# The products of the experts' second matrices as two 64-row tiles of TensorE

## The chip, the cores and the metric

The kernel runs on one core of one Trainium2 chip. Its time is the device time of one execution in microseconds (us); less is better. A core has five engines with instruction queues of their own: TensorE (PE in the profile, with its weight loads listed apart as PEld), VectorE (DVE), ScalarE (ACT), GpSimd (POOL) and SyncE (SP). TensorE multiplies a stationary matrix (the weights, loaded ahead of each product) with a moving one and adds the products up in PSUM, a small memory of eight banks of 128 x 512 floats. Only VectorE and ScalarE read PSUM.

## What is computed

The reference is a sparse attention whose output goes through a mixture of experts with fixed capacity. Cut to what matters:

```python
# attention: q, k, v are (8, 8, 576, 64)
scores = scale * q @ k.T
scores = where(scores >= max(scores) - tau, scores, -1e9)
x = softmax(scores) @ v               # laid out as 4608 tokens x 512
# routing: the best (token, expert) pairs first, 576 tokens for each of 8 experts
logits = x @ w_gate
for idx in argsort(-logits.flatten()):
    tok, e = idx // 8, idx % 8
    if assigned[tok] < 0 and counts[e] < 576: assigned[tok] = e; counts[e] += 1
# experts
for e in range(8):
    h = maximum(x[assigned == e] @ w1[e], 0)      # 576x512 @ 512x1024
    out[assigned == e] = h @ w2[e]                # 576x1024 @ 1024x512
```

## The kernel before

**Two phases.** Until about 480 us attention runs; then come eight rounds, one expert each. A round finds its expert's 576 tokens by a search over thresholds (class `Router`, lines 503 to 547: comparisons on VectorE, counts by small matmuls), gathers their rows (line 780), scales and transposes them (line 806) and runs the two matrices of the expert, `ffn`. Search, gather and transposes of later rounds run while `ffn` of an earlier round keeps TensorE busy, and their small matmuls stand between its products.

**Number format.** Both matrices work on float32 split into a high and a low part (`w1h`, `w1l`, `w2h`, `w2l`, and in `H` the same for the hidden values), each in the reduced format F32R, which TensorE takes in one pass. A product needs three matmuls: high by high, high by low and low by high. Attention works on full float32, which TensorE takes in two passes, each with a record of its own in the trace.

**First matrix.** Line 865: for each of eight blocks of 128 hidden rows, 24 matmuls of mostly 288 columns, into a PSUM tile `pf` of two banks. ScalarE takes the rectified values out (line 877) and rounds them to the high part, VectorE subtracts to get the low part (all VectorE work of this phase has line 426, a helper that also keeps the planner's clock).

**Second matrix.** Line 897: for each of five blocks of 128 tokens, in the order 0, 4, 1, 2, 3 (`L2O`), eight hidden blocks f times three matmuls with all 128 rows and 512 columns, 24 in all, added up in the first bank of a `pf` tile. The other bank lies idle. Block 4 holds the high and the low part of the last 64 tokens side by side and needs 16 matmuls; its halves are added later with the help of a DMA (`y5`, `z5`). Line 900: ScalarE copies the bank to `y`. Line 905: GpSimd issues an indirect DMA that scatters the rows to the output. Eight rounds have 8 x (4 x 24 + 16) = 896 of these matmuls.

**Order of the work.** The program's order on every engine is written out by a planner in the kernel itself: generators yield estimated times, `ffn` is the one that paces the plan, and `jobs` are the others. Small VectorE jobs are put into a list `fills` by `later(key, work)`. A function `flush` takes them out once they are 7 us old or VectorE is free, the search takes one at each of its gaps, and `want(key)` takes one out on the spot when the work that follows needs it. PSUM holds two `pf` tiles (two banks each), two tiles for transposes and two for the search and the packing.

The attention's scores (line 69) already go in two tiles of 64 rows: each of the two matmuls of a head takes 64 of the 128 partitions and a bank of its own.

Of the kernel before, what the change touches and what calls it, by code (L numbers as in the profile page):

```python
# [9 lines left out]
F32 = mybir.dt.float32  # L10
# [4 lines left out]
ALU = mybir.AluOpType  # L15
# [686 lines left out]
def moe(ctx,tc,R,start,xrows,w1,w2,out,ident):  # L702
    nc=tc.nc
    V=R.V; A=nc.scalar; G=nc.gpsimd; T=nc.tensor
    E,D,F=w1.shape
    w1p=ctx.enter_context(tc.tile_pool(name="mw1",bufs=1))
    wk=ctx.enter_context(tc.tile_pool(name="mwk",bufs=1))
# [2 lines left out]
    st={}  # L710
    done=set()

    fills=[]
    def later(k,g): fills.append((clk[0],k,g))
    def pull(k=None):
        if fills:
            i=next((i for i,x in enumerate(fills) if x[1]==k),None)
            if i is None: i=next((i for i,x in enumerate(fills) if x[1][0] in ("hl","w2l","w2")),0)
            _,k,g=fills.pop(i); g(); done.add(k)
# [119 lines left out]
    def ffn(r,s):  # L839
        H=wk.tile([128,8,2*CAP],F32R,name="H")  # L840
        def want(*k):
            while k not in done:
                if any(x[1]==k for x in fills): pull(k)
                else: yield k


        blocks=[(f,(0,1)) for f in range(8)]
        if r==0: blocks[:2]=[(0,(0,)),(1,(0,)),(0,(1,)),(1,(1,))]
        elif r<=HALF: blocks[:1]=[(0,(0,)),(0,(1,))]
        cols=(slice(0,256),slice(256,576)) if r==0 else (slice(0,HS),slice(HS,2*HS))  # L850
        pss={}
        for f,hs in blocks:
            if 0 in hs:
                if r>0 and f==4: yield from want("w1a",r)
                if f>=HFB: yield from want("hl",r,f-HFB)
                pss[f]=pf.tile([128,2,512],F32,name="pf")
            ps=pss[f]
            if hs==(1,): yield ("x",r)
            ops=[(k,j) for j in range(3) for k in range(4)] if r==0 else [(k,j) for k in range(4) for j in range(3)]
            for i,(k,j) in enumerate(ops):  # L860
                w,x=(("w1h","xh"),("w1h","xl"),("w1l","xh"))[j]
                if r==0 and (k,j)==(0,2): yield ("w1l",f)
                for h in hs:
                    n=cols[h].stop-cols[h].start
                    T.matmul(ps[:,h,:n],s[w][:,k,f*128:(f+1)*128],s[x][:,k,cols[h]],start=(i==0),stop=(i==11))  # L865
                if i<11: yield (0.25 if r==0 and hs==(0,) else 0.132)*len(hs)
            if 1 not in hs: yield 0.132; continue
            two=lambda a: a.rearrange("p (a b) -> p a b",a=2)
            hT=two(H[:,f,0:512]); hL=two(H[:,f,512:576]); lL=two(H[:,f,576:640]); lT=two(H[:,f,640:1152])
            hf=wk.tile([128,2,HS],F32,name="hf",bufs=HFB)  # L870
            if r==0:
                hv=hf.rearrange("p a b -> p (a b)")
                hT,hL,lL,lT=H[:,f,0:512],H[:,f,512:576],H[:,f,576:640],H[:,f,640:1152]; v0,v1=hv[:,0:512],hv[:,512:576]
                for h in range(2): A.activation(hv[:,cols[h]],ps[:,h,:cols[h].stop-cols[h].start],AF.Relu)
            else:
                v0,v1=hf[:,:,0:256],hf[:,:,256:288]
                A.activation(hf,ps[:,:,:HS],AF.Relu)  # L877
            A.activation(hT,v0,AF.Copy); A.activation(hL,v1,AF.Copy)
            def low(f=f,a=((lT,hT,v0),(lL,hL,v1))):
                yield LOWT  # L880
                gp=r in LOWP and f<LPF
                def work():
                    for l,h,v in a: (G if gp else V).tensor_tensor(l,v,h.bitcast(F32),op=ALU.subtract)
                if gp: work(); done.add(("hl",r,f))
                else: later(("hl",r,f),work)
            jobs.append([clk[0],low()])
            yield 0.25
        done.add(("l1",r))
        for t in L2O:
            ps=pf.tile([128,2,512],F32,name="pf")  # L890
            ops=(((576-64,"w2h"),(576-64,"w2l")) if t==4 else ((t*128,"w2h"),(t*128,"w2l"),(640+t*128,"w2h")))
            for f in range(8):
                yield from want("hl",r,f)
                yield from want(*(("w2l",r,f) if f<7 else ("w2",r)))
                for j,(c,w) in enumerate(ops):
                    e=(f==7 and j==len(ops)-1)
                    T.matmul(ps[:,0,:],H[:,f,c:c+128],s[w][:,f],start=(f==0 and j==0),stop=e)  # L897
                    if not e: yield 0.227
            y=wk.tile([128,D],F32,name="y5",bufs=1) if t==4 else wk.tile([128,D],F32,name="y",bufs=2)
            A.activation(y,ps[:,0,:],AF.Copy)  # L900
            if t==4:
                if r>0: yield from want("y5",r-1)
                y5=y; z=wk.tile([64,D],F32,name="z5",bufs=1); nc.scalar.dma_start(z,y[64:128])
            def store(t,y,n):
                G.indirect_dma_start(out=out,out_offset=IOA(ap=s["idx"][:n,t:t+1],axis=0),in_=y[:n],in_offset=None)  # L905
            if t<4: store(t,y,128)
            if t==(L2Z if r==7 else 2):
                def last(y5=y5,z=z,store=store):
                    V.tensor_tensor(y5[0:64],y5[0:64],z,op=ALU.add); store(4,y5,64)
                if r==7: last()  # L910
                else: later(("y5",r),last)
            yield 0.227
        done.add(("l2",r))
# [44 lines left out]
    for r in range(8):  # L958
        while not all((n,r) in done for n in ("w1","half" if r<=HALF else "x")):
            now+=0.25; run(now)  # L960
        for d in ffn(r,st[r]):
            if type(d) is tuple:
                while d not in done:
                    now+=0.25; run(now)
                    if d not in done and any(x[1]==d for x in fills): pull(d)
                continue
            held[0]=0.0; now+=d; run(now); now+=held[0]; clk[0]=now
# [35 lines left out]
def build(tc, qk, vl, tau, wgd, cst_d, w1, w2, out, off, nb=8):  # L1003
    nc=tc.nc
    with ExitStack() as ctx:
        ctx.enter_context(tc.manual_schedule())
        cp=ctx.enter_context(tc.tile_pool(name="cst",bufs=1))
        dr=ctx.enter_context(tc.tile_pool(name="dr",bufs=1,space=bass.MemoryType.DRAM))
        xrows=dr.tile([8*S,XW],F32,name="xrows")
        xts=dr.tile([8,128,4,S],F32,name="xts")  # L1010
        ident=cp.tile([128,128],F32,name="ident"); make_identity(nc,ident)
        dup=cp.tile([128,128],F32,name="dup")
        for a in range(2): nc.vector.tensor_tensor(dup[:,64*a:64*a+64],ident[:,0:64],ident[:,64:128],op=ALU.add)
        Lg=cp.tile([128,NC_,8],F32,name="Lg")
        cst=cp.tile(list(cst_d.shape),F32,name="cst")
        R=Router(ctx,tc,cst,off,Lg)
        def load_cst(): nc.sync.dma_start(cst,cst_d)
        with ExitStack() as actx:
            start=attention(actx,tc,qk,vl,tau,wgd,xrows,xts,Lg,nb,ident,dup,R,load_cst)
        pp=ctx.enter_context(tc.tile_pool(name="rp",bufs=1,space=PSUM))  # L1020
        R.ps=lambda t=pp.tile([128,512],F32,name="rps"): t
        R.cp=lambda t=pp.tile([128,512],F32,name="cps"): t
        moe(ctx,tc,R,start,xrows,w1,w2,out,ident)
# [15 lines left out]
```

## Time and profile before

| | |
|---|---|
| time, median of 3 runs | 968.95 us (968.77 to 970.25) |
| the profiled execution | 967.75 us, span 966.0 us |
| mean granted TensorE clock | 0.989 |
| VectorE, ScalarE, GpSimd busy | 80%, 66%, 28% of the span |
| line 900, ScalarE, y from pf | 40 times, 598 ns |
| line 905, output stores on GpSimd | 40 times |
| a round of the experts, rounds 1 to 3 | about 60 us |
| the last round's second matrix | 931 to 956.6 us |

A line of the profile names the source line, the engine, the operation, output and inputs with their shapes, the count, the busy time in us and the mean duration in ns. For TensorE the shape in front, 128\*128 or 64\*128, is the rows and columns of the array that the instruction uses: 64\*128 is a tile of half height. Matmuls overlap in TensorE's pipeline, so a duration is longer than the distance from one start to the next.

### The profile page before, as it was taken

What the parts mean: (1) busy time and instruction counts of PE and PEld (TensorE: products, weight loads), DVE (VectorE), ACT (ScalarE), POOL (GpSimd) and SP (SyncE); (2) the same over time, 40 slices, a digit from 0 to 9 for tenths busy, and PEclk for the clock granted to TensorE, in tenths of its full rate; (3) what the DMA queues carried; (4) which work ended last, traced back from release to release, by engine and by line L of the source; (5) the groups of instructions that cost most, each with busy time, mean ns of one, the idle gap of its engine ahead of it and who ended that gap; (6) DMA issues with size and microseconds to landing.
All of it is one profiled execution on the core that took longest, in us unless ns stands there. A gap on an engine that the chain in (4) does not pass through costs nothing.

```text
span 966.0 us, 24118 instructions
## 1 busy us (share of the span) xinstructions
PE 938.5 (97%) x9130; PEld 700.3 (72%) x9130; DVE 769.8 (80%) x2134; ACT 638.6 (66%) x1297; POOL 269.0 (28%) x485
## 2 busy tenths in 40 slices
PE   7999999999999999999789999999999999999996
PEld 4556656565566656565688798897988979898994
DVE  8999999999999999996678878687887877536220
ACT  6999999999999999996554354342543525455330
POOL 2435344353434343340020412121111212210101
PEclk9999999999999999999889999999999999999998
DMA  6332253532533323205751516143343425431101
GB/s 259 108 115 88 86 184 103 197 134 100 179 101 111 125 100 125 88 2 204 251 169 65 198 59 187 52 138 126 109 149 127 137 95 186 163 98 34 40 12 43
DMA packets 35861, 117.00 MB, mean 121 GB/s; under 512 B 4385, under 2 KB 5025, under 8 KB 35233
## 3 DMA queue, kind: packets, MB, share of 16 engines
q1 hardware_dynamic: 28352, 92.85, 27.6%
q0 software_dynamic: 5888, 19.03, 6.2%
q10 hardware_dynamic: 1504, 3.59, 1.2%
q8 instruction: 72, 1.18, 0.5%
q14 instruction: 45, 0.36, 0.1%
HBM read 93.01 MB, written 21.38 MB: 118 GB/s over the span
## 4 chain that ended last, share of the span: by engine, by line
PE 90%; DVE 5%; DMA 2%; issue 2%; ACT 0%; POOL 0%; POOLq 0%; SPq 0%; DVEq 0%
PE pf L865 22%; PE pf L897 20%; PE sc L69 15%; PE xo L155 14%; PE tb L98 8%; PE sc L98 2%; PE xo L165 2%; PE pt L806 2%; DVE pp L90 1%; PE rps L503 1%; DVE z L74 1%; PE xo L177 1%; PE xo L246 1%; DMA out_dram<-y,idx 1%; DVE cmp L426 1%
## 5 line engine op out<-in xcount | busy, mean ns | idle before, releaser
L74 DVE TENSOR_SCALAR_CACHE_REDUCE z<-sc 128x576 f32<-128x576 f32 x288 | 205.9, 751 | 15.4 <-PE sc L69 13.5
L75 POOL TENSOR_SCALAR nb<-nb,taub 128x1 f32<-128x1 f32 x288 | 145.4, 506 | 248.6 <-DVE z L74 185.5
L86 ACT ACTIVATE pp<-z,nb 128x576 f32<-128x576 f32 x256 | 193.1, 773 | 25.2 <-DVE z L74 22.0
L90 DVE SCALAR_TENSOR_TENSOR pp<-z,nb,pp 128x576 f32<-128x576 f32 x256 | 199.9, 813 | 0.0
L897 PE MATMUL pf<-w2h,H 128*128 128x512 f32 x576 | 193.7, 400 | 0.4 <-DVE H L426 0.4
L69 PE MATMUL sc<-qk 64*128 64x288 f32 (+1 forms) x1280 | 178.6, 423 | 1.5 <-DMA qk<-qk_dram 0.7
L155 PE MATMUL xo<-pt,vt 128*64 128x320 f32 (+1 forms) x1024 | 155.9, 420 | 0.0
L116 ACT ACTIVATE pt<-tb 128x512 f32<-128x512 f32 x253 | 137.6, 591 | 1.9 <-PE tb L98 1.4
L897 PE MATMUL pf<-w2l,H 128*128 128x512 f32 x320 | 128.0, 400 | 0.0
L905 POOL DMA_INDIRECT out_dram<-y,idx x40 | 44.8, 1120 | 295.5 <-ACT y L900 251.1
L897 PEld LDWEIGHTS pf<-w2h,H 128*128 128x128 f32 x576 | 106.7, 188 | 22.1 <-DVE H L426 0.8
L69 PEld LDWEIGHTS sc<-qk 64*128 64x128 f32 (+1 forms) x1280 | 93.7, 178 | 28.8 <-DVE z L74 4.3
L865 PE MATMUL pf<-xl,w1h 128*128 128x288 f32 (+2 forms) x512 | 110.4, 301 | 0.0
L865 PE MATMUL pf<-xh,w1h 128*128 128x288 f32 (+2 forms) x512 | 109.7, 300 | 0.7 <-ACT xh L807 0.7
L865 PE MATMUL pf<-xh,w1l 128*128 128x288 f32 (+2 forms) x512 | 109.7, 300 | 0.0
L98 PEld LDWEIGHTS tb<-ident,pp 64*128 64x128 f32 x2032 | 75.0, 139 | 44.9 <-issue 18.9
L900 ACT ACTIVATE y<-pf 128x512 f32<-128x512 f32 x40 | 23.9, 598 | 124.9 <-PE pf L897 117.0
L155 PEld LDWEIGHTS xo<-pt,vt 128*64 128x64 f32 x1024 | 60.6, 136 | 58.5 <-issue 32.4
L877 ACT ACTIVATE hf<-pf 128x576 f32<-128x576 f32 x56 | 36.5, 652 | 89.1 <-PE pf L865 80.8
L98 PE MATMUL tb<-ident,pp 64*128 64x64 f32 x2032 | 91.7, 227 | 3.3 <-ACT pt L116 3.0
L865 PEld LDWEIGHTS pf<-xh,w1h 128*128 128x128 f32 x512 | 82.1, 189 | 1.8 <-ACT xh L807 1.1
L865 PEld LDWEIGHTS pf<-xl,w1h 128*128 128x128 f32 x512 | 81.9, 190 | 0.2
(201 smaller groups left out, 1316.1 us busy)
## 6 DMA issues: line engine op xcount, KB each, us to landing
qk<-qk_dram SPq DMA_DIRECT2D x31, 864.0 KB, 4.6
vt<-vl_dram SPq DMA_DIRECT2D x32, 576.0 KB, 3.8
w2s<-w_dram SPq DMA_DIRECT2D x32, 512.0 KB, 5.5
w1s<-w_dram SPq DMA_DIRECT2D x28, 512.0 KB, 5.8
xrows<-pp SPq DMA_DIRECT2D x24, 260.0 KB, 2.4
xts<-xt SPq DMA_DIRECT2D x2, 1152.0 KB, 5.4
pt<-xts SPq DMA_DIRECT2D x2, 1152.0 KB, 6.2
xrows<-xr SPq DMA_DIRECT2D x8, 260.0 KB, 2.2
```

Source lines behind the costliest of these rows:

```text
L69: T.matmul(sc[o,f,:HS], kd["q",h][r,c], kd["k",h][r,:],start=True,stop=True)
L74: V.tensor_scalar(z,SC.pop(t)[:,:,:HS],-0.125,None,op0=ALU.mult,op1=ALU.min,accum_out=nb[:,0:1])
L75: G.tensor_scalar(nb[:,1:2],nb[:,0:1],taub[:,0:1],None,op0=ALU.add)
L86: A.activation(pview(t),ZB[t].rearrange("p a b -> p (a b)"),AF.Exp,bias=NBI[t][:,0:1],scale=-1.0)
L90: V.scalar_tensor_tensor(pv,ZB.pop(t).rearrange("p a b -> p (a b)"),NBI[t][:,1:2],pv,op0=ALU.is_le,op1=ALU.mult,accum_out=den_of(p)[:,p%4/ ...
L98: g=slice(64*r,64*r+64); T.transpose(o[:,r],x[r%len(x)][g],ident[g,g])
L116: else: A.activation(o,tb,AF.Copy)
L155: T.matmul(xo[64*h:64*h+64,:q.stop-q.start],v[:,f,128*u+64*h:128*u+64*h+64],PT[p][:,h,u,q],start=new,stop=last,skip_group_check=True)
L865: T.matmul(ps[:,h,:n],s[w][:,k,f*128:(f+1)*128],s[x][:,k,cols[h]],start=(i==0),stop=(i==11))
L877: A.activation(hf,ps[:,:,:HS],AF.Relu)
L897: T.matmul(ps[:,0,:],H[:,f,c:c+128],s[w][:,f],start=(f==0 and j==0),stop=e)
L905: G.indirect_dma_start(out=out,out_offset=IOA(ap=s["idx"][:n,t:t+1],axis=0),in_=y[:n],in_offset=None)
```

## The change

In every block of the second matrix but block 4, and but the very last block of the last round, each matmul of 128 rows is replaced by two of 64 rows: rows 0 to 63 add up in the first bank of the `pf` tile, rows 64 to 127 in the second. ScalarE copies the first bank to `y` as before. A new VectorE operation adds the second bank to `y`, and the store follows it; both go into `fills` under the key `("ya", r, t)`. Before a `pf` tile is taken, the add of the tile two before it is asked for by `want` (`pend` keeps the keys), since its buffer is taken over. In the last block of the last round the add of the block before it is asked for at the fifth hidden block. `y` gets three buffers in place of two.

That makes 8 x 4 - 1 = 31 tiled blocks. The planner's times stay as they are (0.227 us for a product, now for a pair).

```diff
+    fills=[]; pend=[]
...
             if 0 in hs:
                 if r>0 and f==4: yield from want("w1a",r)
                 if f>=HFB: yield from want("hl",r,f-HFB)
+                if len(pend)>1 and pend[-2]: yield from want(*pend[-2])
+                pend.append(None)
                 pss[f]=pf.tile([128,2,512],F32,name="pf")
...
         for t in L2O:
+            tiled=t<4 and not (r==7 and t==L2O[-1])
+            if len(pend)>1 and pend[-2]: yield from want(*pend[-2])
+            pend.append(("ya",r,t) if tiled else None)
             ps=pf.tile([128,2,512],F32,name="pf")
...
             for f in range(8):
                 yield from want("hl",r,f)
+                if r==7 and t==L2O[-1] and f==4: yield from want("ya",7,L2O[-2])
...
                     e=(f==7 and j==len(ops)-1)
-                    T.matmul(ps[:,0,:],H[:,f,c:c+128],s[w][:,f],start=(f==0 and j==0),stop=e)
+                    if tiled:
+                        for a in range(2):
+                            g=slice(64*a,64*a+64)
+                            T.matmul(ps[:,a,:],H[g,f,c:c+128],s[w][g,f],start=(f==0 and j==0),stop=e)
+                    else: T.matmul(ps[:,0,:],H[:,f,c:c+128],s[w][:,f],start=(f==0 and j==0),stop=e)
                     if not e: yield 0.227
...
-            if t<4: store(t,y,128)
+            if tiled:
+                def add(t=t,y=y,ps=ps,store=store):
+                    V.tensor_tensor(y,y,ps[:,1,:],op=ALU.add); store(t,y,128)
+                later(("ya",r,t),add)
+            elif t<4: store(t,y,128)
```

More of the change, by code (lines that the diff above doesn't have):

```diff
@@ L711, in moe @@
     done=set()
-    fills=[]
+    fills=[]; pend=[]
     def later(k,g): fills.append((clk[0],k,g))
@@ L896, in ffn @@
                     e=(f==7 and j==len(ops)-1)
-                    T.matmul(ps[:,0,:],H[:,f,c:c+128],s[w][:,f],start=(f==0 and j==0),stop=e)
+                    if tiled:
[3 more added lines that the diff above has]
+                    else: T.matmul(ps[:,0,:],H[:,f,c:c+128],s[w][:,f],start=(f==0 and j==0),stop=e)
                     if not e: yield 0.227
-            y=wk.tile([128,D],F32,name="y5",bufs=1) if t==4 else wk.tile([128,D],F32,name="y",bufs=2)
+            y=wk.tile([128,D],F32,name="y5",bufs=1) if t==4 else wk.tile([128,D],F32,name="y",bufs=3)
             A.activation(y,ps[:,0,:],AF.Copy)
```

## The prediction

> **What bounds the kernel now.** I read the page first: the engines' shares, the TensorE clock and the chain of waits.
>
> ```profile
> span 966.0 us, 24118 instructions
> PE 938.5 (97%) x9130; PEld 700.3 (72%) x9130; DVE 769.8 (80%) x2134; ACT 638.6 (66%) x1297; POOL 269.0 (28%) x485
> PE 90%; DVE 5%; DMA 2%; issue 2%; ACT 0%; POOL 0%; POOLq 0%; SPq 0%; DVEq 0%
> L897 PE MATMUL pf<-w2h,H 128*128 128x512 f32 x576 | 193.7, 400 | 0.4 <-DVE H L426 0.4
> L897 PE MATMUL pf<-w2l,H 128*128 128x512 f32 x320 | 128.0, 400 | 0.0
> ```
>
> TensorE (PE) is 90% of the chain, and line 897, which the change rewrites, has 576+320=896 matmuls with 0.4 us of waiting in front of them. An average can hide a stage, so next came the table of windows for one round of the experts (617 to 677 us) and PE's own waits from 524 to 957 us.
>
> ```profile
> 617.00:677.00 60.00, 60.00 (x443) 51.90 (x444) 47.06 (x129) 25.55 (x52) 11.12 (x11) 1.00 0.33 112
> PE pf L897 <- DVE H L426: 0.4, 1, 0.4
> ```
>
> The columns after the window are its length and the busy time of PE, PEld, DVE, ACT and POOL, then the granted clock. PE is covered for the whole 60 us at clock 1.00, while DVE has 12.9 us free. So in this stage each nanosecond that PE's stream gets longer or shorter goes straight into the time; I look for nothing else until PE is done.
>
> A busy time of 400 ns is not the price of a matmul, since they are pipelined. The price is the distance from start to start, which I take from the longest unbroken pieces of the chain in order of time (start, length, count).
>
> ```profile
> 905.61 25.59 PE pf L865 x192
> 931.20 14.56 PE pf L897 x64
> ```
>
> A 288-column matmul costs 25.59/192=0.1333 us, a 512-column one 14.56/64=0.2275. The difference is 0.0942 for 224 columns, 0.000421 us a column; 288 columns stream in 0.1211, so 0.0122 us is left at every matmul whatever its length. This fixed part is the only thing that two half-height tiles could win, if they run side by side: each still streams all 512 columns.
>
> **The change part by part: the pair.** 31 of the 40 blocks are tiled, 24 products each: 744 matmuls become 744 pairs. No row shows the reduced float format in a 64-row tile. The nearest in shape are the attention's scores, two 64-row tiles in full float; the timeline gives:
>
> ```profile
> 203.06 0.65 PE L69 MATMUL sc<-qk 64*128 64x288 f32 x4
> 203.30 0.65 PE L69 MATMUL sc<-qk 64*128 64x288 f32 x4
> ```
>
> Each row begins at one pair, so a pair takes 203.30-203.06=0.24 us for 288 columns, and the two tiles do run together. That is 2.0 times 288 x 0.000421=0.121: a full-float pass streams a column in two column times, and nothing of a fixed part is visible. So the price of a new pair lies between 0.2275-0.0122=0.2153 (by the scores: 744 x 0.0122=9.1 us won) and 0.2275 (by line 897 itself). I take 0.2275, no gain. What has no fixed part need not owe it to the tiles: four full-height transposes, quoted below, start (0.60-0.273)/3=0.109 us apart for 128 columns, 2.0 times 128 x 0.000421=0.054, in full float too, untiled, and again with next to no fixed part. The 0.0122 goes with the format, not with the height of the tile, and the change keeps the format.
>
> **The switches.** PE does not stay in one shape. Between the products of line 897 stand the small matmuls of the later rounds' search (L503, L515, L533, L547) and the row transposes (L806), almost all full height. Once line 897 is half height, each such visit changes the shape twice. Before the change two kinds of visit already do so, and the timeline prices them. First four half-height transposes:
>
> ```profile
> 889.63 0.39 PE L897 MATMUL pf<-w2h,H 128*128 128x512 f32 x1
> 889.95 0.46 PE L806 MATMUL pt<-ident,xg 64*128 64x64 f32 x4
> 890.34 0.50 PE L897 MATMUL pf<-w2h,H 128*128 128x512 f32 x1
> 890.68 0.39 PE L897 MATMUL pf<-w2l,H 128*128 128x512 f32 x1
> ```
>
> Then four full-height ones, and the mean durations of both kinds:
>
> ```profile
> 548.00 0.62 PE L897 MATMUL pf<-w2h,H 128*128 128x512 f32 x2
> 548.46 0.60 PE L806 MATMUL pt<-ident,xg 128*128 128x128 f32 x4
> 548.81 0.48 PE L897 MATMUL pf<-w2l,H 128*128 128x512 f32 x1
> 549.13 0.63 PE L897 MATMUL pf<-w2h,H 128*128 128x512 f32 x2
> L806 PE MATMUL pt<-ident,xg 128*128 128x128 f32 x112 | 14.9, 273 | 0.0
> L806 PE MATMUL pt<-ident,xg 64*128 64x64 f32 x28 | 3.2, 235 | 0.0
> ```
>
> Half height: from 889.63 to 890.68 are 1.05 us, two products (0.455) and the visit: 0.595. Its own four matmuls take 0.22 (half of 0.109 each) to 0.30 ((0.46-0.235)/3=0.075 each), so 0.295 to 0.375 is the price of going there and back. Full height: 549.13-548.00=1.13 with three products (0.6825) leaves 0.4475, its own 4 x 0.109=0.436 and 0.01 over. A transposing visit thus gains about 0.33 us when it must change shape. The same for short matmuls, a quarter-height pair:
>
> ```profile
> 735.19 0.62 PE L897 MATMUL pf<-w2h,H 128*128 128x512 f32 x2
> 735.74 0.17 PE L533 MATMUL rps<-jka,hb 32*128 32x1 bf16 x1
> 735.78 0.16 PE L540 MATMUL rps<-jka,onesb 32*128 32x9 bf16 x1
> 735.88 0.50 PE L897 MATMUL pf<-w2l,H 128*128 128x512 f32 x1
> 736.21 0.39 PE L897 MATMUL pf<-w2h,H 128*128 128x512 f32 x1
> ```
>
> Against a single full-height one:
>
> ```profile
> 553.41 0.39 PE L897 MATMUL pf<-w2h,H 128*128 128x512 f32 x1
> 553.64 0.18 PE L533 MATMUL rps<-fla,hb 128*128 128x1 bf16 x1
> 553.68 0.48 PE L897 MATMUL pf<-w2h,H 128*128 128x512 f32 x1
> 553.99 0.40 PE L897 MATMUL pf<-w2l,H 128*128 128x512 f32 x1
> ```
>
> 1.02-0.6825=0.3375 against 0.58-0.455=0.125; the second small matmul is 0.04 of it (735.78-735.74), so 0.17 us is the price here. It is less, because a visit of short matmuls already leaves the next weights uncovered.
>
> The Trainium skill, on the page "TensorEngine Tiling (Array Packing)", section "Tiling Modes", says that going to another tiling mode, not merely to another tile, drains TensorE. It gives no figure; the two prices above are what it costs here, so the trace agrees, and the rule speaks against this change.
>
> How many visits? The table of windows over the 16 stretches of tiled blocks (block 0 and blocks 1 to 3 of each round, in the last round 1 and 2), asked for one line at a time; the first row shows one stretch of L503, the others are the sums for L503, L515, L533, L547, L540 and L806.
>
> ```profile
> 585.20:591.80 6.60, 0.39 (x9) 1.00 0.24 55
> sum 194.81, PE 7.80; mean PE 0.49
> sum 194.81, PE 3.33; mean PE 0.21
> sum 194.81, PE 2.30; mean PE 0.14
> sum 194.81, PE 1.05; mean PE 0.07
> sum 194.81, PE 0.32; mean PE 0.02
> sum 194.81, PE 12.93; mean PE 0.81
> ```
>
> L503 comes in nines of 0.39: 7.80/0.39=20 visits. L515, L533 and L547 are single matmuls of about 0.17: 20, 13 and 6. Two of L515 and one of L547 stand next to transposes, and two of L533 go with the two L540 (0.32/0.16), which change shape already: 18, 11 and 5 are left. In all 54 visits x 0.17=9.2 us. L806: seven half-height fours (7 x 0.46=3.2) and, in the other 9.7 us, eleven full-height visits (about seven eights of 1.03 and four fours of 0.60). The eleven cost 11 x 0.33=3.6; the seven now meet a matching height and give back 7 x 0.33=2.3.
>
> The blocks themselves switch too. Block 4 stays untiled between block 0 and block 1, and the first matrix is full height: four changes a round and four in the last, 32 one-way changes. At half of 0.33 that is 5.3 us (bounds: half of 0.17 and half of 0.375, 2.7 and 6.0).
>
> **The added work off TensorE.** The add is shaped like this group:
>
> ```profile
> L426 DVE TENSOR_TENSOR xl<-pt,xh 128x512 fp32r<-128x512 f32 x28 | 18.5, 678 | 0.9 <-ACT xh L807 0.9
> ```
>
> 31 adds x 0.68=21.1 us of DVE, four a round (2.7 us) against the 12.9 us free in 617 to 677, so no cost; if PE had to wait for each, it would be 21.1 us. Two waits are new. The block after next needs the PSUM tile whose second bank DVE reads, so PE's queue (that block, and the search matmuls behind it) waits if the add is late; but a whole block, 24 x 0.2275=5.5 us, lies between, eight times the add. And DVE may sit on the add until ScalarE has written y, with the search's comparisons behind it; the search has rounds in hand. The output store now follows the add on POOL, with 5.5 us of cover as well, and the last block is untiled, so the end of the kernel keeps its order. ScalarE's copy and the number of stores don't change; the third y tile costs no instruction. I take nothing for all this.
>
> **Sum.** 9.2+3.6-2.3+5.3=15.8 us longer (12.5 to 17.2 with the bounds of the switches), pairs and DVE at nothing. The profiled execution took 967.75 us, its span of 966.0 and 1.75 around it; that is 1.2 below the median of 968.95, about as much as the three runs lie apart (968.77 to 970.25). From it the sum gives 983.55 (967.75+15.8), from the median 984.75, so I forecast 984.8.
>
> **The rivals.** *The pair loses its fixed part, and the switches are paid*: 15.8-9.1=6.7 longer, 975.7. For it: the scores' pairs at 0.24. Against: the untiled transposes have no fixed part either. On the page "TensorE: Matmul & The Clock Gate", Part 3, section "The mechanism", the Trainium skill says that a weight load overlaps running matmuls only where its row group differs, by which tiles would hide what full-height products expose. The trace shows otherwise for most of a load:
>
> ```profile
> L897 PEld LDWEIGHTS pf<-w2h,H 128*128 128x128 f32 x576 | 106.7, 188 | 22.1 <-DVE H L426 0.8
> ```
>
> A load of 0.188 us has no room between products that start 0.2275 apart and stream for 0.2153.
>
> *Faster: the fixed part goes and the switches are nearly free*, because two half-height tiles drain and reload one behind the other, so that one tile streams while the other changes. Then 9.1 us are won, 959.9. It decides at 9.1/15.8: if a switch costs under 58% of my prices, the kernel gets faster. Against it: at both priced visits the next product came late by the whole price.
>
> *The tiles do not run side by side in this format*, so that the change does not do what it says: a second stream at each product, 744 x 0.2275=169 us, 1154. Against it stand only the full-float pairs.
>
> *DVE becomes the bound*: its queue holds adds back and PE waits at each third block; with half to all of the 21.1 us, 995 to 1006. Against it: 12.9 us free in each round.
>
> **How the numbers follow.** Forecast 0.51; fixed part gone and switches paid 0.22; faster 0.14; serial tiles 0.05; DVE 0.08. A change of 0.2%, 1.9 us, is about what a measurement of this kernel can tell from none. Faster by more than that takes nearly the whole third case, 0.12; within it 0.05, from the meeting of the second and third; slower 0.83. The range from 966 to 998 leaves out most of the faster case (0.12), the serial one (0.05) and the upper half of the DVE case (0.03).
>
> **What would show it.** The spacing of pairs in the last rounds, where no visit disturbs them: 0.227 for me, 0.215 for the rivals, 0.45 for serial tiles. A visit of nine L503 in a tiled block: 0.17 longer than before. The first product of a tiled block: 0.15 to 0.2 late behind line 865. PE waits on DVE's add near nothing. I am wrong if PE's spacing at the switches hardly changes, or if PE waits for DVE in front of blocks.

## The result and the profile after

The changed kernel takes 992.67 us (median of 6 runs, 992.14 to 994.02), the kernel before 969.60 (6 runs on the same chip): 23.1 us more, a ratio of 1.0242 (95% interval 1.0230 to 1.0254). The forecast was 984.8 us with a range of 966 to 998, slower. The sign and the kind of cost are as forecast; of the 23.1 us the sum had 15.8.

In the page of the changed kernel line 906 is the pairs, 907 the products that stay whole, 867 the first matrix, 910 ScalarE's copy, 915 the store. First its span and engines, the chain by engine, and the larger group of the pairs:

```profile
span 990.7 us, 25636 instructions
PE 959.7 (97%) x9874; PEld 708.0 (71%) x9874; DVE 790.2 (80%) x2165; ACT 638.9 (64%) x1297; POOL 263.9 (27%) x485
PE 90%; DVE 4%; DMA 2%; issue 2%; ACT 1%; POOL 0%; POOLq 0%; SPq 0%; ACTq 0%; DVEq 0%
L906 PE MATMUL pf<-w2h,H 64*128 64x512 f32 x992 | 170.7, 403 | 2.8 <-ACT y L910 2.7
```

PE is still 90% of the chain, and its busy time grew by 21.2 us (959.7-938.5). The 31 adds stand in DVE's x2165 (2134+31). New is the 2.7 us of waiting for line 910's copy.

**The spacing of the pairs.** From the timeline of the last round, where nothing stands between the products:

```profile
970.54 0.62 PE L906 MATMUL pf<-w2h,H 64*128 64x512 f32 x4
...
971.22 0.62 PE L906 MATMUL pf<-w2h,H 64*128 64x512 f32 x4
```

Between the two rows lie three pairs (the row left out holds one): (971.22-970.54)/3=0.2267 us. Whole products start as far apart (0.2275 in the piece of 64 quoted before). The tiles run side by side, and they win nothing.

**A block's end.** The same round, where block 0 (tiled) ends and block 4 (whole) begins:

```profile
960.30 0.39 PE L906 MATMUL pf<-w2h,H 64*128 64x512 f32 x2
960.61 0.50 PE L907 MATMUL pf<-w2h,H 128*128 128x512 f32 x1
960.95 0.40 PE L907 MATMUL pf<-w2l,H 128*128 128x512 f32 x1
```

0.65 us for two products; 0.65-2x0.2267=0.20 is what one change of shape costs there. The chain of the last round, cut by line, shows the whole price:

```profile
929.18 25.80 PE pf L867 x192
954.98 5.71 PE pf L906 x48
```

Piece one, the first matrix, took 25.59 before: 0.21 more. Piece two, block 0, is 24 pairs in 5.71, where 24x0.2267 is 5.44: 0.27 more. So beside the two products at the change, the next ones also run a little apart.

**A visit.** Nine matmuls of line 503 inside a tiled block, in the timeline of after:

```profile
667.75 0.39 PE L906 MATMUL pf<-w2l,H 64*128 64x512 f32 x2
668.07 0.39 PE L503 MATMUL rps<-oh,cmp 128*128 128x32 bf16 x9
668.39 0.73 PE L906 MATMUL pf<-w2h,H 64*128 64x512 f32 x4
668.96 0.40 PE L906 MATMUL pf<-w2l,H 64*128 64x512 f32 x2
```

And in the kernel before:

```profile
649.25 0.39 PE L897 MATMUL pf<-w2l,H 128*128 128x512 f32 x1
649.48 0.39 PE L503 MATMUL rps<-oh,cmp 128*128 128x32 bf16 x9
649.72 0.70 PE L897 MATMUL pf<-w2h,H 128*128 128x512 f32 x2
650.26 0.40 PE L897 MATMUL pf<-w2l,H 128*128 128x512 f32 x1
```

Less three products (0.68), the visit takes 0.53 now and took 0.33: 0.20 more. The nine start 0.09 later behind the last product (0.32 against 0.23) and the next product 0.08 later behind them (0.32 against 0.24): both ends of the visit pay. The forecast had 0.17. A single matmul (line 547, in the tiled block 0 at 596.27) takes 0.32 us once three products are taken off (1.00 from 595.72 to 596.72), where the prediction's single visit took 0.125: 0.19 more. Eight full-height transposes of line 806 in a tiled block take 1.34 us from the product before them to the next one (670.56 to 671.90), and took 1.02 in the kernel before (656.20 to 657.22): 0.32 more.

**Half-height transposes** now meet half-height products:

```profile
913.50 0.62 PE L906 MATMUL pf<-w2h,H 64*128 64x512 f32 x4
913.96 0.28 PE L806 MATMUL pt<-ident,xg 64*128 64x64 f32 x2
914.02 0.50 PE L906 MATMUL pf<-w2l,H 64*128 64x512 f32 x1
914.08 0.29 PE L806 MATMUL pt<-ident,xg 64*128 64x64 f32 x2
914.18 0.47 PE L906 MATMUL pf<-w2l,H 64*128 64x512 f32 x1
914.36 0.76 PE L906 MATMUL pf<-w2h,H 64*128 64x512 f32 x4
```

The two matmuls of one pair, elsewhere together, start at 914.02 and 914.18: while four transposes pass through one tile, the other goes on with its product. From 913.50 to 914.36 are two pairs and the next one, 0.86-3x0.2267=0.18 for this visit, where it was 0.595 in the kernel before.

**In front of block 1.** The table of PE's waits of the changed kernel (us in total, times, longest) has two new lines that the adds bring:

```profile
PE pf L906 <- ACT y L910: 2.7, 4, 0.7
PE pf L867 <- DVE y L426: 0.6, 1, 0.6
```

The second is one wait for an add itself, in front of a block of the first matrix. The first are four places, one in each of the rounds 1 to 4 (rounds count from 0), all between block 4 and block 1. The timelines of PE, ACT and DVE at the first:

```profile
597.05 0.50 PE L907 MATMUL pf<-w2h,H 128*128 128x512 f32 x1
...
600.24 0.39 PE L907 MATMUL pf<-w2h,H 128*128 128x512 f32 x1
600.47 0.17 PE L515 MATMUL rps<-c8n,sum 128*32 128x8 f32 x1
600.50 0.48 PE L907 MATMUL pf<-w2l,H 128*128 128x512 f32 x1
600.82 0.40 PE L907 MATMUL pf<-w2h,H 128*128 128x512 f32 x1
601.05 0.40 PE L907 MATMUL pf<-w2l,H 128*128 128x512 f32 x1
602.13 0.50 PE L906 MATMUL pf<-w2h,H 64*128 64x512 f32 x2 [0.69 <-ACT y L910]
```

```profile
601.49 0.60 ACT L910 ACTIVATE y<-pf 128x512 f32<-128x512 f32 x1 [2.68 <-PE pf L907]
```

```profile
600.47 1.28 DVE L426 TENSOR_TENSOR xg<-xg 128x512 f32<-128x512 f32 x2
...
601.76 0.67 DVE L426 TENSOR_TENSOR w1l<-w1s,w1h 128x512 fp32r<-128x512 f32 x1
602.36 0.67 DVE L426 TENSOR_TENSOR y<-y,pf 128x512 f32<-128x512 f32 x1
```

Block 4's last product starts at 601.05, its copy runs from 601.49 to 602.09, and block 1 starts at 602.13, 1.08 behind. The add of block 0 stands in DVE's order behind two row scalings and a weight's low part and runs at 602.36, after block 1 has begun. A pair writes both banks of its tile, and the add still has to read block 0's second bank. So block 1 is not in block 0's tile: it has taken the tile of the block just finished, and waits for its copy. Beyond a spacing (0.23) this costs 0.85 us, more than the 0.69 that the row gives as a wait. The 0.10 that a first product behind a change of shape starts late anyway (0.33 behind the last) lies within it.

### The profile page after: what moved, and what is told of

Read it like the earlier page. It is cut to its first block, busy times and chain, and to the rows that moved or that the text cites. A ratio compares the mean times of both kernels' runs of the same rounds, so it can differ in the third digit from the quotient of the medians.

```text
span 990.7 us, 25636 instructions
## 1 busy us (share of the span) xinstructions
PE 959.7 (97%) x9874; PEld 708.0 (71%) x9874; DVE 790.2 (80%) x2165; ACT 638.9 (64%) x1297; POOL 263.9 (27%) x485
## 4 chain that ended last, share of the span: by engine, by line
PE 90%; DVE 4%; DMA 2%; issue 2%; ACT 1%; POOL 0%; POOLq 0%; SPq 0%; ACTq 0%; DVEq 0%
PE pf L867 21%; PE pf L906 19%; PE sc L69 14%; PE xo L155 14%; PE tb L98 8%; PE pf L907 3%; PE sc L98 2%; PE xo L165 2%; PE pt L806 2%; PE rps L503 1%; DVE pp L90 1%; DVE z L74 1%; PE xo L177 1%; PE xo L246 1%; DVE cmp L426 1%
## 5 line engine op out<-in xcount | busy, mean ns | idle before, releaser
L906 PE MATMUL pf<-w2h,H 64*128 64x512 f32 x992 | 170.7, 403 | 2.8 <-ACT y L910 2.7
L915 POOL DMA_INDIRECT out_dram<-y,idx x40 | 41.4, 1036 | 310.3 <-DVE y L426 259.2
L906 PEld LDWEIGHTS pf<-w2h,H 64*128 64x128 f32 x992 | 99.6, 184 | 22.1 <-ACT y L910 4.2
L906 PE MATMUL pf<-w2l,H 64*128 64x512 f32 x496 | 106.9, 400 | 0.0
```

The source lines that it names most:

```text
L906: T.matmul(ps[:,a,:],H[g,f,c:c+128],s[w][g,f],start=(f==0 and j==0),stop=e)
```

## The experiments

Lines are of the changed kernel where nothing else is said, and the difference is to it. Ratios are to the kernel before in the same session; it took 968.91, 973.44, 968.91 and 968.06 us in the four of them, so kernels of different sessions are compared by ratio. A difference in us is between the medians of one session.

**Are adds and order guilty, or the tiles?** Two kernels take the change apart. In the first the products stay whole but still go to two banks, half the hidden blocks to each, with the add, its waits and the late store:

```diff
-                    if tiled:
-                        for a in range(2):
-                            g=slice(64*a,64*a+64)
-                            T.matmul(ps[:,a,:],H[g,f,c:c+128],s[w][g,f],start=(f==0 and j==0),stop=e)
+                    if tiled: T.matmul(ps[:,f//4,:],H[:,f,c:c+128],s[w][:,f],start=(f%4==0 and j==0),stop=(f%4==3 and j==len(ops)-1))
```

> The changed kernel with the tiles taken back: the 24 products of a block keep all 128 rows, those of hidden blocks 0 to 3 add up in the first bank, those of 4 to 7 in the second; the 31 VectorE adds, the wait for them and the later store stay. Theory (the time goes to TensorE's changes of shape, about 0.2 us one way): 971 to 975 us, since only the waits for the add in front of block 1 stay, about 0.8 us in four rounds. Rival (the adds and what they hold up cost the time): about 990 us. Rival (a pair is dearer than a product): 970 us.

Measured: 974.69 us, ratio 1.0054 (1.0039 to 1.0070): 5.8 us by the medians, 5.2 by the ratio. PE's waits show the same line as the changed kernel:

```profile
PE pf L903 <- ACT y L907: 2.7, 4, 0.7
```

So the adds are not free, and the stall in front of block 1 belongs to them and not to the tiles. The four lie in rounds 1 to 4; the last rounds, where the search has run out, show none. The one wait of 0.6 us for an add is there too. At 0.85 us a stall these come to 4.0 us; the rest, 1 to 2 us, has no wait to its name.

The second keeps the pairs and leaves the adds out (the second bank never reaches the output), with the store right behind the copy:

```diff
-            pend.append(("ya",r,t) if tiled else None)
+            pend.append(None)
...
-                if r==7 and t==L2O[-1] and f==4: yield from want("ya",7,L2O[-2])
...
-                    V.tensor_tensor(y,y,ps[:,1,:],op=ALU.add); store(t,y,128)
-                later(("ya",r,t),add)
+                    store(t,y,128)
+                add()
```

> The changed kernel without the adds: the pairs stay, the second bank is computed and left out of the output, the store follows ScalarE's copy as before the change. Theory (changes of shape): 988 to 990 us, the changed kernel's 992.7 less the 3 to 4 us of waiting for the add. Rival (adds): about 970 us.

Measured: 988.95 us, ratio 1.0201 (1.0185 to 1.0216): 20.0 us for the tiles alone (19.5 by the ratio), and no wait on the copy or on an add is left among PE's waits. 20.0 and 5.8 make 25.8, 19.5 and 5.2 make 24.7, against 23.1 for both together: within what the intervals leave open (1.5 us on each side of either) they add up.

**Are the tiles' 20 us changes of shape?** If so, they go with the number of changes and not with the number of pairs. First tiles in the last three rounds alone, where few visits stand between the products:

```diff
-            tiled=t<4 and not (r==7 and t==L2O[-1])
+            tiled=r>4 and t<4 and not (r==7 and t==L2O[-1])
```

> The changed kernel with tiles only in rounds 5 to 7, where hardly any search is left between the products: 11 of 31 tiled blocks, 264 of 744 pairs, 11 of 31 adds. Theory (changes of shape): 12 at block ends x 0.2 = 2.4 us, two visits of full-height transposes +0.34 each, two of half-height ones -0.48 each: 2.1 us over the kernel before, 971.7 us. Rival (cost goes with the number of pairs or adds): 264/744 or 11/31 of 23.1 us, 8.2 us over, 977.8 us.

Measured: 971.99 us, ratio 1.0031 (1.0019 to 1.0043), 3.1 us. 11 of the 31 tiled blocks, 35%, bring 3.1/20.0=15% of the tiles' loss: not a price for each pair. Twelve block ends at 0.27 are 3.2.

Then, in the same rounds, every other hidden block whole:

```diff
+            tiled=r>4 and t<4 and not (r==7 and t==L2O[-1])
...
-                    if tiled:
+                    if tiled and f%2:
...
-                            T.matmul(ps[:,a,:],H[g,f,c:c+128],s[w][g,f],start=(f==0 and j==0),stop=e)
+                            T.matmul(ps[:,a,:],H[g,f,c:c+128],s[w][g,f],start=(a==1 and f==1 and j==0),stop=e)
```

> As the kernel with tiles in rounds 5 to 7, but in a tiled block only the odd hidden blocks go as pairs (132 pairs in all), the even ones as full-height products into the first bank: half the pairs, the same adds, eight changes of shape in a block, 88 in all in place of 12. Theory (changes of shape): 88 x 0.2 = 17.6 us over the kernel before, 987 us. Rival (pairs): 132/744 of 23.1 us, 4.1 over, 973.7 us. Rival (adds): 977.8 us, as with tiles in the last three rounds.

Measured: 987.95 us, ratio 1.0196 (1.0180 to 1.0211), 19.0 us with half the pairs of the run before. 88 changes: 19.0/88=0.22 us each. Against the run before, which has the same adds, 76 changes more cost 16.0 us, 0.21 each. Its timeline:

```profile
951.34 0.40 PE L907 MATMUL pf<-w2h,H 128*128 128x512 f32 x1
951.67 0.50 PE L906 MATMUL pf<-w2h,H 64*128 64x512 f32 x2
952.01 0.40 PE L906 MATMUL pf<-w2l,H 64*128 64x512 f32 x2
...
952.57 0.50 PE L907 MATMUL pf<-w2h,H 128*128 128x512 f32 x1
```

From 951.67 to 952.57 are 0.90 us for three pairs (the row left out is the third), 0.22 more than 3x0.2267. The change comes in two halves: the first product of the new shape starts 0.10 late (0.33 behind the last), and the second 0.11 late (0.34 behind the first), as at the block ends. The Trainium skill, page "TensorEngine Tiling (Array Packing)", section "Tiling Modes", says that going to another mode drains TensorE; this trace agrees for a change of height, at 0.22 us. For a change of width alone the traces show no such price (last section).

**Does the fixed 0.0122 us belong to the format?** In the last round the blocks take other formats (the last expert's output isn't computed): block 0 bf16 whole, block 4 the reduced format, block 1 bf16 in pairs, block 2 full float whole, block 3 full float in pairs. This kernel ran once, and only distances inside its trace are read.

```diff
+            tiled=r==7 and t in (1,3); FM={0:BF16,1:BF16,2:F32,3:F32}.get(t) if r==7 else None
...
+                    hh=H[:,f,c:c+128]; ww=s[w][:,f]
+                    if FM is BF16: hh=R.ones; ww=R.cmp[:,0:512]
+                    elif FM is F32: hh=hh.bitcast(F32); ww=ww.bitcast(F32)
...
```

> A kernel for one look, in which nothing is tiled but in the last round the second matrix runs each block in another form, 24 products of 512 columns each: block 0 in bfloat16 at full height, block 1 in bfloat16 as pairs of tiles, block 4 as before, block 2 in full float at full height, block 3 in full float as pairs (the bfloat16 operands are tables of the search, so the last expert's output is not computed). What is read is the distance from start to start. Theory (the 0.012 us over the streaming goes with the reduced format and not with the height): 0.2155 for bfloat16 in both heights, 0.431 a pass for full float in both heights, 0.2275 for block 4. Rival (it goes with full-height products, and tiles hide it): 0.2275 and 0.443 at full height, 0.2155 and 0.431 as pairs.

Its timeline, for bf16 and full float, whole (line 910) and in pairs (line 909):

```profile
934.97 5.35 PE L910 MATMUL pf<-cmp,onesb 128*128 128x512 bf16 x24
943.90 5.35 PE L909 MATMUL pf<-cmp,onesb 64*128 64x512 bf16 x48
951.01 1.88 PE L910 MATMUL pf<-w2h,H 128*128 128x512 f32 x4
953.58 1.88 PE L910 MATMUL pf<-w2h,H 128*128 128x512 f32 x4
971.80 1.88 PE L909 MATMUL pf<-w2h,H 64*128 64x512 f32 x8
974.38 1.88 PE L909 MATMUL pf<-w2h,H 64*128 64x512 f32 x8
```

24 bf16 products take 5.35 us whole and in pairs. Less about 0.39 for the last one's own duration, that is 23 spacings of 0.216, which is 512 columns at 0.000421. A full-float product, two passes, takes (953.58-951.01)/3=0.857 whole and 2.58/3=0.860 in pairs, 0.429 or 0.430 a pass: twice 0.2156=0.431, so a pass takes two column times for each column. Neither has the 0.0122, in either height; the reduced format has it in either height. What the rival read out of the scores' pairs was their format.

**Where do the adds lose their time?** Four kernels move the add or the blocks. First the add right behind ScalarE's copy, in place of `later`:

```diff
-                later(("ya",r,t),add)
+                add(); done.add(("ya",r,t))
```

> The changed kernel with each add and store issued right behind ScalarE's copy in place of the list of small jobs. Theory: TensorE no longer waits in front of block 1, 992.7 less about 3.5 us: 989 us, unless VectorE, which now stands still until ScalarE has written y, holds back the search. Rival (VectorE's load, not the moment of the add, makes TensorE wait): 992 us or more.

Measured: ratio 1.0215 (1.0190 to 1.0239), hardly apart from the changed kernel's 1.0242 (1.0230 to 1.0254). The wait in front of block 1 is gone, and another has come, of the search on VectorE's comparison:

```profile
PE rps L515 <- DVE c8n L426: 2.7, 3, 1.6
```

VectorE now sits behind the copy (its waits for ScalarE's y grow from 37.5 us in the changed kernel to 54.4, from 500 to 985 us), and the search behind VectorE. The prediction had said that "the search has rounds in hand"; here it hasn't.

Next block 4 first, so that all tiled blocks follow each other and two of four changes a round fall away:

```diff
-W1Y=5.0; L2O=(0,4,1,2,3); L2Z=1; HFB=3; RW=[0.2,0.4,0.4,0.4]; LOWP=(); LPF=7; LOWT=1.4; PREPW=1; WLY=(1.0,1.0)
+W1Y=5.0; L2O=(4,0,1,2,3); L2Z=1; HFB=3; RW=[0.2,0.4,0.4,0.4]; LOWP=(); LPF=7; LOWT=1.4; PREPW=1; WLY=(1.0,1.0)
```

> The changed kernel with block 4 first in place of second, so that blocks 0 to 3 follow one another: two changes of shape less in each round, 16 in all, and the block that waits for an add has a long block ahead of it. Theory (changes of shape): 16 x 0.2 = 3.2 us, and the 3 us of waiting in front of block 1, less than 992.7: 986.5 us. Rival (cost goes with pairs): 992 us.

Measured: ratio 1.0358 (1.0331 to 1.0386), slower by over 1% where a gain was expected. PE's waits say why:

```profile
PE pf L907 <- DVE H L426: 7.9, 6, 2.6
PE pf L906 <- DVE y L426: 4.0, 3, 2.4
```

Block 4 needs the high and the low parts of the last tokens' hidden values, and as the first block it now waits for VectorE to make them; adds come late on top. The same order in the kernel before, with nothing else changed:

> The kernel before with block 4 first, the control for the same order in the changed kernel: no shape changes, no adds, so 969 us by every theory; what it differs from 969 is what the order costs by itself.

Measured: ratio 1.0049 (1.0032 to 1.0066), and the first of the two waits is there, halved:

```profile
PE pf L897 <- DVE H L426: 3.7, 3, 2.6
```

So the order costs 0.5% by itself. The rest goes with waits that only the order together with tiles and adds brings: 4.2 us more on H and 4.0 on the adds. In round 6, where neither kernel lists a wait of PE, the order does save: from one start of the first matrix to the next are 53.92 us (891.59 to 945.51 in the chain), in the changed kernel 54.41 (874.77 to 929.18), 0.49 for two changes fewer, or 0.24 each; without tiles the round takes 53.46 in either order. Over the whole, fewer changes bring nothing if the order that has them starves PE.

Then the add of the block before is asked for ahead of ScalarE's copy, so that it stands earlier in the program:

```diff
+            if pend[-2]: yield from want(*pend[-2])
             A.activation(y,ps[:,0,:],AF.Copy)
```

> The changed kernel with one more demand: the add of the block before is put into VectorE's order ahead of ScalarE's copy of the present block, so that the two PSUM tiles come free in the order in which they were taken. Theory (block 1 waits in four rounds because it takes over the tile of block 4, whose copy is just being made, and not because VectorE is full): the 2.7 us of waiting go, 990 us against 992.7. Rival (VectorE's load): 992 us or more, with TensorE waiting for the add itself.

Measured: ratio 1.0248 (1.0228 to 1.0268), no change, and PE's waits on the copy stay at 2.7 us in four places. The theory that the written order of add and copy decides which tile block 1 takes over has fallen. On the same chip the changed kernel itself, unaltered, gave this:

> The changed kernel itself, once more, on the chip of the two others and in the same rounds, so that they can be compared with it: 1.024 times the kernel before by every theory.

Measured: 993.38 us, ratio 1.0256 (1.0233 to 1.0279).

Last, the add of block 0 is asked for in the middle of block 4, after its copy and ahead of the row scalings in DVE's order:

```diff
                 if r==7 and t==L2O[-1] and f==4: yield from want("ya",7,L2O[-2])
+                if t==4 and f==3: yield from want(*pend[-2])
```

> The changed kernel, with one more line: at the fourth hidden block of block 4 the add of block 0 is asked for, so that it stands in VectorE's order before block 4 ends, and late enough that ScalarE's copy of block 0 (0.60 us) is over. Theory: the four stalls of about 0.8 us in front of block 1 come from the place of the add in VectorE's order; then they go, PE's waits on line 910's copy with them, and the time falls by about 3 us, ratio to the kernel before about 1.021. Rival A: an earlier add only pushes the search's comparisons and the next weights' low parts back by the same time, as the add at once did (a wait of L515 on VectorE of 2.7 us came in its place): ratio stays 1.024 to 1.026. Rival B: block 1 takes over block 4's tile whatever the add does: the waits on the copy stay at 2.7 us, ratio 1.025.

Measured: 991.06 us, ratio 1.0234 (1.0217 to 1.0251). The waits on the copy are gone. Timelines of PE, ACT and DVE at the same place (lines one higher):

```profile
600.39 0.40 PE L908 MATMUL pf<-w2l,H 128*128 128x512 f32 x1
600.72 0.50 PE L907 MATMUL pf<-w2h,H 64*128 64x512 f32 x2
```

```profile
600.83 0.60 ACT L911 ACTIVATE y<-pf 128x512 f32<-128x512 f32 x1 [2.69 <-PE pf L908]
```

```profile
597.98 0.68 DVE L426 TENSOR_TENSOR y<-y,pf 128x512 f32<-128x512 f32 x1
```

The add is over at 598.66; block 1 starts 0.33 behind block 4's last product, the price of the change alone, and ahead of block 4's copy: it now takes block 0's tile. The place of the add in VectorE's order is what made the stall. Yet the four stalls, 0.75 us each beyond the price of the change, bring back only 1 to 2 us (from 1.0242 and 1.0256 to 1.0234, intervals that overlap), short of the 3 expected. PE's waits show part of the reason: the wait of 0.6 us on an add in front of the first matrix has gone as well, but one of 0.7 on ScalarE's rectified values and one of 0.4 on another add have come.

**The rule turned round.** If a visit costs by its change of height, the kernel before gains where its own half- and quarter-height visits become full height. There the transposes of the last 64 rows run over 128 (the rest set to zero), and lines 533 and 540 take 128 rows of a zero-filled `jka`:

```diff
-                k=32 if l==5 else 128
+                k=128
...
-            s.T.matmul(ps[:,1:10],s.ones[0:32],s.jk,start=True,stop=True)
+            s.T.matmul(ps[:,1:10],s.ones,s.jk,start=True,stop=True)
...
+            if t==4: V.e.memset(x[64:128,0:D],0.0)
...
-            for d in range(4): T.transpose(ps[:,d,:n],s["xg",t][:n,d*128:(d+1)*128],ident[:n,:n])
+            for d in range(4): T.transpose(ps[:,d],s["xg",t][:,d*128:(d+1)*128],ident)
```

> The kernel before, with the shape changes that it already has in the experts' phase taken out: the transposes of the last 64 rows are done at full height (the 64 unused rows are set to zero by VectorE) and the two matmuls of 32 rows in the search (lines 533 and 540) at full height too (GpSimd sets the unused rows to zero). Theory (a change of shape costs about 0.2 us one way): a visit of half-height transposes 0.59 becomes 0.45, eight times, and the search's pair 0.34 becomes 0.17, seven times: 1.1 + 1.2 = 2.3 us less than the kernel before, 0.24%. Rival (the price is that of half-height matmuls as such): full height is as dear or dearer, no change.

Measured: 966.85 us (12 runs) against 968.91 (17 runs), ratio 0.9978 (0.9967 to 0.9988): 2.1 us faster, and faster than both kernels of this study. Its timeline at the visit that the prediction priced:

```profile
888.57 0.39 PE L898 MATMUL pf<-w2h,H 128*128 128x512 f32 x1
888.80 0.60 PE L807 MATMUL pt<-ident,xg 128*128 128x128 f32 x4
...
889.47 0.39 PE L898 MATMUL pf<-w2l,H 128*128 128x512 f32 x1
```

0.90-2x0.2267=0.45 us for twice the columns, where the half-height visit took 0.595. The 2.1 us hold both savings, of the transposes and of the search's pairs. Of the pairs, the one at 787.65 takes 0.17 in place of 0.34; the one at 734.97 has to wait 0.9 us for the `jka` that GpSimd fills with zeros.

## Why the prediction was right, and where its sizes were off

**Pairs at 0.2275, no gain: right.** 0.2267 in the last round, and the formats show that the 0.0122 us belongs to the reduced format and not to the height.

**Short visits, 54 x 0.17=9.2: mechanism right, a little small.** The nine of line 503 grew by 0.20, a single matmul by 0.19; at 0.20 the 54 are 10.8.

**Full-height transposes, 11 x 0.33=3.6: right.** The eight quoted above cost 0.32 more, and in the trace of after eleven such visits stand between tiled products.

**Half-height transposes, 7 x -0.33=-2.3: right in sign, too small.** They don't just lose their change of shape, they run beside the other tile: 0.595-0.18=0.42 each in the visit quoted, 2.9.

**Block ends, 32 x 0.165=5.3: mis-sized.** Half of a there-and-back price missed what the following products lose. By the pieces of the last round one is 0.21 to 0.27, so 6.7 to 8.6, beyond the bound of 6.0.

The four together are 10.8+3.6-2.9+8.6=20.1 (18.2 by the lower block end), against the prediction's 15.8 (12.5 to 17.2) and the 20.0 us of the tiles alone.

**"I take nothing for all this": the step that failed.** The adds cost 5.2 to 5.8 us with whole products, and 3 to 4 on top of the tiles (23.1-20.0=3.1, or 1.0242-1.0201=0.0041 by the ratios). The prediction let "a whole block, 24 x 0.2275=5.5 us" lie between a block and the one that needs its tile. In front of block 1 that block is block 4, 16 products, started within 4.0 us (597.05 to 601.05), and the add stands late in VectorE's order behind work of other jobs. DVE's 12.9 us free in a round say nothing on when they are free. The wait there came not on the add but on the copy of block 4, whose tile block 1 took instead. The prediction named as a sign of its error "if PE waits for DVE in front of blocks". PE did wait in front of blocks: once for DVE's add (0.6 us), and four times for ScalarE's copy, because an add came late. Nor did the search have "rounds in hand", as the run with the add at once showed.

Of the rivals, the gain of the fixed part is ruled out by the spacing, serial tiles too, and VectorE as the bound of the whole is not seen: the adds' loss is about a quarter of the 23.1 us at most. Open are the 1 to 2 us of the adds' loss that no wait shows, and what chooses the tile that block 1 takes over; the runs show only that it follows VectorE's order, not the order of the program's lines around the copy.

## What to carry to other kernels

Before you tile a stretch of TensorE, count what else passes through it: between products of 0.227 us a visit of short matmuls that changes the array's height and back costs about 0.2 us more than one that doesn't, a visit of transposes 0.33, and a one-way change at a block's end 0.2 to 0.27. So 54 small visits and 32 block ends outweigh a gain of 0.0122 us on 744 products even if that gain were there. Where small matmuls must pass between large ones, give them the height of the large ones, padding with zeros if needed. Cover for a new operation on a partly idle engine is measured at the shortest block and at its place in that engine's order, not by the engine's free time in a round.

## What the runs showed of the hardware

- Small matmuls of the same height as the tiles can pass through one tile while the other keeps streaming: the four half-height transposes at 913.96 cost 0.18 us in place of 0.595.
- A change of the width alone shows no price here. Line 515 works on 128\*32, and its visit in the whole block 4 quoted above (600.24 to 600.82, 0.58 less 0.455) costs 0.125, as much as the full-width visit of line 533 in the prediction.
- Of the three formats, only the reduced float has the fixed part of 0.0122 us a matmul. Whole and in pairs, bf16 takes 0.000421 us a column and full float twice that in each pass, with nothing over.
